# Fused attention and mixture of experts: tables ahead of scatters, maxima transposed in score banks, other places and another engine for weight loads, later last logits

## The chip, the cores and the metric

The kernel runs on one core of a Trainium2 chip, as one program from the attention's inputs to the mixture's output. The metric is the device time of one execution in microseconds (us), taken over several runs of the same kernel. The engines are named as in the profile: PE (TensorE, with PEld for its weight loads), DVE (VectorE), ACT (ScalarE), POOL (GpSimd) and SP (SyncE, which here does little but issue DMAs).

## The reference

```python
scores = (q @ k.T) / sqrt(64)                       # 8 batches, 8 heads, S = 576, D = 64
scores = where(scores >= max(scores) - 0.02, scores, -1e9)
attn = softmax(scores) @ v                          # sum + 1e-9 below
x = attn.transpose(0, 2, 1, 3).reshape(4608, 512)   # tokens x (head, d)
logits = x @ w_gate                                 # 8 experts
e = argmax(logits); gate = softmax(logits)[e]       # one expert per token
for e in range(8):
    h = relu(x[mask_e] @ w1[e])                     # 512 -> 1024
    out[mask_e] = gate * (h @ w2[e])                # 1024 -> 512
```

## The kernel before

**Attention.** The 64 heads are 32 pairs n = 0 to 31, four pairs to a batch b = 0 to 7. Products are exact to about f32 by splitting each f32 operand in two f16 parts (hi, lo) and summing three products. A pair takes NSTEP = 11 steps k. In a step PE makes one score tile `s` (queries on the partitions, for the row maxima, `s_unit`) of a later pair and one transposed score tile `st` (`st_unit`) of the pair at hand, and `av_piece` multiplies masked exponentials with v. `st_unit` makes e = exp on ACT, masks it on DVE, casts it to f16 (`ph`) on ACT and takes the low part (`pl`) on POOL. The maxima of a pair reach the transposed scores through `parts`: DVE reduces them to `r`, PE transposes `r` into a PSUM tile `pst`, ACT and DVE split that in three f16 parts `ptT`, and SP copies them to rows 64 to 66 of the pair's operand tile `CQ`. A pair's operands QK, ck, CQ are in one of four sets, used in turn.

**From attention to experts.** `finish(b)` divides by the sums and writes the tokens of a batch as rows `R`; SP transposes them to `xTg`; `logits(b)` multiplies with the gate's weights (tile `lg`), `route(b)` finds maximum, one-hot expert (`oh`) and the running counts per expert (`run`), all on DVE, and `ranks` places each token by matmuls with `before` and `ones` (`rk`), and POOL scatters the rows by indirect DMA to the table `xs` in DRAM, sorted by expert (`send`). For b = 5, 6, 7 tables follow (`tables0`, `tables1`, `tables2`: counts `cnt`, places `row`, from PE's `pc`), then `fetch(m)` gathers 128 rows of an expert by an indirect DMA on POOL (`Rm`, `spare`, later `R`) and transposes them by a DMA on SP (`xTm`). `lg`, `pst`, `rk`, `pc` all stand in one PSUM bank, tile "m" of the pool `ps_m`; score tiles, and the identity products `hi_v`, `hi_w` that help splitting, use the pool `ps_sc` (tile "sc", six banks).

**Experts.** Weights come in as f32 chunks `wf` (e, w, c) of 512 KB (`load_w`; w = 0 or 1 for w1 or w2, c = 0 to 3), eight for an expert, and `split_w` makes hi and lo parts `wb1`, `wb2` with ACT (hi) and DVE (lo). `gemm1` gives h = relu(x w1) in 96 matmuls of 128 columns for a block of 128 tokens, split in `hl` (ACT, DVE); `gemm2` gives y in 24 matmuls of 512 columns, scaled by the gate (`o`, ACT) and scattered to the output by POOL. Expert 0 (e0) has four early blocks, m = 0 to 3, whose tokens come from batches 0 to 6; m = 3 and 4 sit in the tile `spare`.

**What sets the order.** The Python loop over k writes the instructions; `plan(k, f)` puts an action at a step, `after(k, f)` at so many steps from now, `chain` spreads a list of small operations over steps (or keeps it in one step with `at_once`), `hurry` raises its priority. Pieces of the gemms are mixed into the attention's steps from step KM = KEND - km at the share rate / 100 a step, then one a step from KEND = 352; `moe(c, ready, f)` runs loads, splits and fetches at a chunk number c of that stream. Then a scheduler with a simulated timeline orders each engine's instructions by priority; what is marked `keep_in_program_order` keeps its place. The table TUNE holds the numbers: `lg7` the steps from the last batch's rows to its logits, `w1a`, `w1b` the chunk at which e1's splits begin and their distance, `w1d` the distance of e1's loads, which `close` begins.

Lines: `parts` 370 to 396, `logits` 551, `route` 576, `ranks` 605, `load_w` 789, `split_w` 804, `fetch` 822, `tables0` to `tables2` 1048 to 1063, `close` 1083, the plan of e0's loads and splits 1090 to 1097.

Of the kernel before, what the change touches and what calls it, by code (L numbers as in the profile page):

```python
# [9 lines left out]
F16 = mybir.dt.float16  # L10
# [7 lines left out]
P = 128  # L18
# [26 lines left out]
TUNE = dict(  # L45
    lead=10, cast=2, sl=8, ll=15, sp0=3, sps=0, lv=-16, sv0=-6, sv1=2, av=2, g=4, l=3, d=4, g5=4, l5=3, d5=2, g6=1, l6=2, d6=2, g7=1, l7=1, d7=1, off=2, off5=1, off6=5, lg=4, lg7=14, km=16, rate=15, dh=1, do=3, ws0=6, wsd=2, w1d=5, plv=1, xv=5, so=0, sto=0, ord=0, sc=6, fa=3, fd=4, wa1=-70, wa2=-86, wl1=-28, wl2=-6, avb=1, route=1, ranks=7, pp=8, ew=4, maskat=0, w1a=-42, w1b=5,
)
# [3 lines left out]
def kernel(  # L51
# [55 lines left out]
    NQ = 4  # L107
    cks = [[cpool.tile([P, S], F16, name=f"ck_{i}_{a}") for a in range(2)] for i in range(NQ)]
    cqs = [op.tile([P, 9 * P], F16, tag=f"CQ{i}", name=f"CQ_{i}", bufs=1) for i in range(NQ)]
    none = before[96:96 + NM, 0:64]  # L110
# [80 lines left out]
    def after(k, f, where=END):  # L191
        plan(now[0] + k, f, where)
# [177 lines left out]
    def parts(n):  # L370
# [18 lines left out]

# [186 lines left out]
    def route(b, n, dist, Lj, w, got):  # L576
# [28 lines left out]
        def ranks(dist=dist):  # L605
# [441 lines left out]

    def tables0():
        T[0] = level("0", ((), EARLY[0]), None)
        for m in range(NF):  # L1050
            after(1 + m, lambda m=m: fetch(m))

    def tables1():
        T[1] = level("1", EARLY, T[0])
        for m in range(2):
            after(1 + m, lambda m=m: fetch(NF + m))

    def tables2():
        cnt, s_e = level("2", (EARLY[1], None), T[1])
# [246 lines left out]
```

## Time and profile before

| | us |
|---|---|
| median of 3 runs | 1001.75 (998.88 to 1005.34) |
| the profiled execution | 997.49 |
| its span in the trace | 995.8 |
| PE busy | 941.6 (95% of the span) |
| DVE, ACT, POOL busy | 700.4, 654.1, 563.1 |
| mean granted PE clock | 0.983 of full speed |

Attention runs to about 585 us and the experts to the end; from about 540 to 660 us they overlap, and batches 6 and 7 are routed. Times in the trace are microseconds from the span's start. An idle time in brackets is that of the engine just before the instruction, with what released it. The rows are below.

### The profile page before, as it was taken

The numbers are of one execution on the slowest core, as the hardware profiler recorded it, in microseconds if no ns is written. First come the engines' busy times: TensorE is split into PE (matmuls) and PEld (weight loads), VectorE is DVE, ScalarE is ACT, GpSimd is POOL, SyncE is SP. The second block draws the span as 40 slices with busy tenths as digits, with TensorE's granted clock in tenths as the row PEclk, the third lists the DMA queues.
The fourth block names the chain that finished last, engine by engine and source line by source line (L and its number), as shares of the span: only waits on it lengthen the run. The fifth ranks groups of instructions, "written<-read, shape, count | busy, mean of one in ns | idle before, by whom it ended". The sixth has DMA issues, their size and how long they took to land. (4 is left out here: it accounts for less than half of the span.)

```text
span 995.8 us, 28654 instructions
## 1 busy us (share of the span) xinstructions
PE 941.6 (95%) x11548; PEld 606.9 (61%) x11548; DVE 700.4 (70%) x1413; ACT 654.1 (66%) x1114; POOL 563.1 (57%) x470
## 2 busy tenths in 40 slices
PE   7899999999999999999998998799999999999997
PEld 2355556556566555565664675677666776667684
DVE  7899999989999889999999664816342333423560
ACT  2689897988989888989989853534243332433651
POOL 6366886895986977969969851343122121221121
PEclk8899999999999999999999899999999999999999
DMA  7553454464555646546636569998664756556630
GB/s 199 146 137 75 140 141 134 121 170 113 148 153 137 160 96 175 146 113 161 150 91 193 88 171 276 379 188 247 170 218 116 224 151 180 164 156 214 217 109 27
DMA packets 142750, 159.20 MB, mean 160 GB/s; under 512 B 96403, under 2 KB 112789, under 8 KB 142614
## 3 DMA queue, kind: packets, MB, share of 16 engines
q1 hardware_dynamic: 126598, 100.33, 39.9%
q0 software_dynamic: 9248, 29.45, 9.1%
q10 hardware_dynamic: 6768, 27.55, 8.8%
q8 instruction: 92, 1.51, 0.6%
q14 instruction: 44, 0.36, 0.1%
HBM read 90.24 MB, written 19.44 MB: 110 GB/s over the span
## 5 line engine op out<-in xcount | busy, mean ns | idle before, releaser
L430 POOL TENSOR_TENSOR pl<-e,ph 128x1024 f16<-128x1024 f32 x158 | 335.8, 2133 | 102.3 <-ACT ph L429 64.0
L421 ACT ACTIVATE e<-st,ntau 128x512 f32<-128x512 f32 (+1 forms) x352 | 222.7, 649 | 53.0 <-PE st L405 49.2
L424 DVE SCALAR_TENSOR_TENSOR e<-st,e 128x512 f32<-128x512 f32 (+1 forms) x352 | 220.3, 636 | 11.2 <-ACT e L421 10.5
L947 PE MATMUL y<-wb,hl 128*128 128x512 f16 (+1 forms) x1056 | 202.9, 361 | 0.0
L368 DVE TENSOR_REDUCE nm<-s 128x1 f32<-128x512 f32 x300 | 188.4, 633 | 20.4 <-PE s L358 18.4
L914 PEld LDWEIGHTS <-wb 128*128 128x128 f16 x2304 | 189.4, 98 | 19.8 <-issue 1.5
L914 PE MATMUL h<-xTm,wb 128*128 128x256 f16 (+2 forms) x2112 | 194.7, 253 | 1.0 <-DMA xTm<-Rm 1.0
L474 PE MATMUL av<-vop,ph 128*128 128x65 f16 (+3 forms) x3072 | 187.9, 195 | 2.3 <-ACT x L484 2.0
L474 PEld LDWEIGHTS <-ph 128*128 128x128 f16 (+1 forms) x3072 | 158.8, 100 | 46.4 <-issue 21.7
L474 PE MATMUL av<-vop,pl 128*128 128x65 f16 (+1 forms) x1536 | 167.8, 194 | 5.4 <-POOL pl L430 5.2
L429 ACT CAST ph<-e 128x1024 f16<-128x1024 f32 x160 | 166.3, 1039 | 6.1 <-DVE e L424 5.7
L474 PEld LDWEIGHTS <-pl 128*128 128x128 f16 (+1 forms) x1536 | 137.1, 100 | 37.0 <-issue 11.2
L947 PEld LDWEIGHTS <-hl 128*128 128x128 f16 (+1 forms) x1056 | 94.2, 100 | 98.6 <-issue 3.0
L817 DVE SCALAR_TENSOR_TENSOR wb<-wf,wb 128x1024 f16<-128x1024 f32 x88 | 103.9, 1221 | 56.3 <-ACT wb L809 54.8
L404 PE MATMUL st<-QK 128*128 128x512 f16 (+3 forms) x640 | 139.3, 296 | 1.5 <-DVE lo L255 0.8
L405 PE MATMUL st<-CQ,ck 128*128 128x512 f16 (+3 forms) x640 | 137.8, 290 | 0.5 <-DMA CQ<-ptT 0.5
L356 PE MATMUL s<-QK 128*128 128x512 f16 (+1 forms) x600 | 129.1, 292 | 2.9 <-DMA QK<-hi 2.1
L358 PE MATMUL s<-ck,CQ 128*128 128x512 f16 (+1 forms) x600 | 127.6, 288 | 1.5 <-DMA CQ<-hi 1.5
L961 POOL DMA_INDIRECT out_dram<-o,gt x40 | 47.8, 1194 | 138.6 <-ACT o L958 128.1
L809 ACT ACTIVATE wb<-wf 128x1024 f16<-128x1024 f32 x96 | 98.0, 1050 | 35.5 <-DMA wf<-in_w_dram 18.6
L902 ACT ACTIVATE hl<-h 128x512 f16<-128x512 f32 (+1 forms) x80 | 45.8, 572 | 109.9 <-PE h L914 108.3
L865 DVE COPY gt<-R 128x1 f32<-128x1 f32 x33 | 5.0, 153 | 129.7 <-DMA out_dram<-o,gt 112.5
(195 smaller groups left out, 1018.4 us busy)
## 6 DMA issues: line engine op xcount, KB each, us to landing
wf<-in_w_dram SPq DMA_DIRECT2D x96, 512.0 KB
qkf<-in_qk_dram ACTq DMA_DIRECT2D x30, 576.0 KB
vf<-in_v_dram ACTq DMA_DIRECT2D x15, 640.0 KB
QK<-hi SPq DMA_DIRECT2D x64, 144.0 KB
QK<-lo SPq DMA_DIRECT2D x64, 72.0 KB
QK<-hi SPq DMA_DIRECT2D x64, 72.0 KB
ck<-lo SPq DMA_DIRECT2D x64, 72.0 KB
CQ<-hi SPq DMA_DIRECT2D x64, 64.0 KB
```

The costliest lines, as they stand in the source:

```text
L356: nc.tensor.matmul(sc[rows, oc], d["QA"][a][:, cols], d["KB"][a][:, CH[c]], start=True, stop=False)
L358: nc.tensor.matmul(sc[rows, oc], d["CQ"][:, at:at + cols.stop - cols.start], d["CK"][a][:, CH[c]], start=False, stop=True,)
L368: nc.vector.tensor_reduce(o, sc[:, 0:width(t)], axis=AX.X, op=ALU.max, negate=True)
L404: nc.tensor.matmul(sc[rows, oc], d["KB"][a][:, cols], d["QA"][a][:, CH[c]], start=True, stop=False)
L405: nc.tensor.matmul(sc[rows, oc], d["CK"][a][:, cols], d["CQ"][:, q], start=False, stop=True)
L421: nc.scalar.activation(pf, sc, AF.Exp, bias=ntau, scale=0.125 / SS)
L424: nc.vector.scalar_tensor_tensor(pf, sc, 0.0, pf, ALU.is_ge, ALU.mult)
L429: nc.scalar.copy(h, pd)
L430: (nc.vector if (n, t) in PLV else nc.gpsimd).tensor_tensor(l, pd, h, ALU.subtract)
L474: nc.tensor.matmul(av[:, 0:D] if z == 2 else av, l if z == 1 else h, vop[:, tv, W:W + D] if z == 2 else vop[:, tv, 0:W], start=i in (0, NT ...
L914: nc.tensor.matmul(o, Wt[:, c, wh, f], x, start=c == 0 and z == 0, stop=c == 3 and z == 2,)
L947: nc.tensor.matmul(o, h[:, hh], Wt[:, f, wh, c], start=f == 0 and z == 0, stop=f == 7 and z == 2)
```

## The change

- **TUNE**: `lg7` 14 to 22 (the last batch's logits eight steps later), `km` 16 to 12 and `rate` 15 to 40 (where and how thickly gemm pieces are mixed into attention's last steps), `w1d` 5 to 4, `w1a` -42 to -38, `w1b` 5 to 4.
- **Operand sets**: the four `ck` and four `CQ` tiles become two tiles each of two sets (`ck2`, `cq2`), so that one tile is large enough for a 512 KB chunk.
- **Maxima**: the last two pairs transpose into a score bank (`ps_sc`) and not bank "m"; for the last pair the chain follows in the same step and with priority.
- **Tables**: `ranks` calls `tables0` and `tables1` five steps after it, ahead of part of the scatters, with a lag so that the fetches stay behind; the last batch's `ranks` come 6 steps after `route`, not at once.
- **Loads**: e0's last two chunks of w2 go into the operand sets of pairs 28 and 29 (`ck2[0]`, `cq2[0]`) and are planned at steps 332 and 333; its w2 splits at steps 353, 355, 357, 359 (before 353, 355, 361, 364). ScalarE issues e1's eight loads, SP the others.

```diff
-lg7=14, km=16, rate=15, w1d=5, w1a=-42, w1b=5
+lg7=22, km=12, rate=40, w1d=4, w1a=-38, w1b=4
...
+    ck2 = [cpool.tile([P, 2, 2, S], F16, name=f"ck_{i}") for i in range(NQ // 2)]
+    cq2 = [op.tile([P, 2, 9 * P], F16, tag=f"CQ{i}", name=f"CQ_{i}", bufs=1) for i in range(NQ // 2)]
...
-            ps = ps_m.tile([P, 512], F32, tag="m", name=f"pst_{n}")
+            pool, tag = (ps_sc, "sc") if n >= NPAIR - 2 else (ps_m, "m")
+            ps = pool.tile([P, 512], F32, tag=tag, name=f"pst_{n}")
...
-            chain(1, [
+            chain(int(n < NPAIR - 1), [
...
-            ])
+            ], n == NPAIR - 1)
...
-        (after if n >= 1 else lambda k, f: hurry(f)())(1, turn)
+        if n == 0:
+            hurry(turn)()
+        else:
+            after(1, hurry(turn) if n == NPAIR - 1 else turn)
...
-                after(wait + dist * n, TABLES[b])
+                at = 5 if b < B - 1 else wait
+                after(at, lambda: TABLES[b](wait + dist * n - at))
...
-        after(0 if b == B - 1 else RK[b], ranks)
+        after(6 if b == B - 1 else RK[b], ranks)
...
+        if (e, w) == (0, 1) and c >= 2:
+            wf = (ck2, cq2)[c - 2][0]
...
+            wq[e, w, c] = wf = wf.bitcast(F32)[:, 0:F]
+            nc.sync.dma_start(wf, w12[e, :, c, w])
+            return
...
-            load = nc.sync.dma_start(wf, w12[e, :, c, w])
+            load = (nc.scalar if e == 1 else nc.sync).dma_start(wf, w12[e, :, c, w])
...
-            after(1 + m, lambda m=m: fetch(m))
+            after(lag + 1 + m, lambda m=m: fetch(m))
...
-        t = k + WS0 + WSD * i if i < 4 else KEND + (1, 3, 9, 12)[i - 4]
+        t = k + WS0 + WSD * i if i < 4 else KEND + 1 + 2 * (i - 4)
...
+            plan(NSTEP * (NPAIR - 2) + i - 4, lambda i=i: load_w(*wseq[i]))
-    TABLES = {B - 3: hurry(tables0), B - 2: tables1, B - 1: tables2}
+    TABLES = {B - 3: tables0, B - 2: tables1, B - 1: tables2}
```

**Place 1, PE where the last pair's maxima are transposed.** Before, `pst_31` stands behind 59 matmuls of `av_29_0`, with score tiles 2 and 3 of pair 30 well ahead of it:

```order
L474 LDWEIGHTS pl_29_2_11930
L474 MATMUL av_29_0_12357<-vop_0_127,pl_29_2_11930 128x65
L474 LDWEIGHTS ph_29_2_11929
L474 MATMUL av_29_0_12357<-vop_0_127,ph_29_2_11929 128x64
L379 MATMUL pst_31_12343<-ident_94,r_31_12326 9x128
L474 LDWEIGHTS ph_29_8_12002
L474 MATMUL av_29_1_12553<-vop_0_127,ph_29_8_12002 128x65
```

Now it stands behind 22 matmuls of `av_29_0`, and pair 30's score tiles 2 and 3 come after it:

```order
L480 MATMUL av_29_0_12355<-vop_0_119,ph_29_0_11901 128x65
L480 LDWEIGHTS pl_29_0_11902
L480 MATMUL av_29_0_12355<-vop_0_119,pl_29_0_11902 128x65
L382 MATMUL pst_31_12335<-ident_94,r_31_12318 9x128
L410 LDWEIGHTS QK_30_0_11134
L410 MATMUL st_30_2_12345<-QK_30_0_11134 128x512
L411 LDWEIGHTS ck_1_116
L411 MATMUL st_30_2_12345<-CQ_1_118,ck_1_116 128x512
L410 LDWEIGHTS QK_30_0_11134
L410 MATMUL st_30_3_12371<-QK_30_0_11134 128x512
```

The transpose moved forward by 37 matmuls of `av_29_0` and by score tiles 2 and 3 of pair 30, which now stand behind it. The first half of `lg_6` (24 matmuls), which stood after score tile 9 of pair 30, now stands ahead of it, right behind score tile 1.

**Place 2, SP where e0's last and e1's loads were.** The names are `wf_` expert, chunk, w1 or w2 (0 or 1). Before:

```order
L794 DMA wf_0_2_1_12999<-in_w12_dram 128x1024
L794 DMA wf_0_3_1_13052<-in_w12_dram 128x1024
L794 DMA wf_1_0_0_13373<-in_w12_dram 128x1024
L860 DMA_TRANSPOSE spare_13218<-spare_13218 128x8x128 x2
L860 DMA_TRANSPOSE xTm_5_13555<-Rm_5_13554 128x8x128
L860 DMA_TRANSPOSE xTm_6_13890<-Rm_6_13889 128x8x128
L543 DMA_TRANSPOSE xTg_7_0_13430<-R_129 128x8x128 x2
L794 DMA wf_1_1_0_13469<-in_w12_dram 128x1024
L543 DMA_TRANSPOSE xTg_7_2_13473<-R_129 128x8x128 x2
L543 DMA_TRANSPOSE xTg_7_4_13506<-R_129 128x8x128
L794 DMA wf_1_2_0_13546<-in_w12_dram 128x1024
L794 DMA wf_1_3_0_13572<-in_w12_dram 128x1024
```

Now, from the fetches of blocks 3 and 4 (`spare`) to the first load of e2:

```order
L873 DMA_TRANSPOSE spare_13240<-spare_13240 128x8x128
L549 DMA_TRANSPOSE xTg_7_0_13444<-R_121 128x8x128 x2
L873 DMA_TRANSPOSE spare_13240<-spare_13240 128x8x128
L873 DMA_TRANSPOSE xTm_5_13543<-Rm_5_13542 128x8x128
L549 DMA_TRANSPOSE xTg_7_2_13491<-R_121 128x8x128 x2
L549 DMA_TRANSPOSE xTg_7_4_13520<-R_121 128x8x128
L873 DMA_TRANSPOSE xTm_6_13774<-Rm_6_13773 128x8x128
L807 DMA wf_2_0_0_13674<-in_w12_dram 128x1024
```

No load stands between the transposes any more; e0's last two chunks stand further ahead in SP's row, right behind `xTg_6_0`, and e1's are with ACT, between the operations of batch 7's rows:

```order
L807 DMA wf_1_1_0_13463<-in_w12_dram 128x1024
L822 ACTIVATE wb1_1_13390<-wf_1_0_0_13393 128x1024
L915 ACTIVATE hl_2_0_13468<-h_2_0_13397 128x512
L541 CAST R_121<-xn_7_2_13440 128x4x128
L541 CAST R_121<-xn_7_3_13461 128x4x128
L915 ACTIVATE hl_2_0_13468<-h_2_1_13471 128x512
L822 ACTIVATE wb1_1_13390<-wf_1_1_0_13463 128x1024
L541 CAST R_121<-xn_7_4_13487 128x4x128
L807 DMA wf_1_2_0_13534<-in_w12_dram 128x1024
L807 DMA wf_1_3_0_13557<-in_w12_dram 128x1024
L807 DMA wf_1_0_1_13573<-in_w12_dram 128x1024
L971 ACTIVATE o_0_0_13575<-y_0_0_13538,gt_0_0_12521 128x512
```

Each load of e1 now stands behind ACT's own work ahead of it, no more behind SP's transposes.

**Place 3, DVE where the last batch is routed.** `lg_7` to `run` is the route of batch 7, `wb2_1` the splits of e1's w2, `wb1_0` those of e2's w1. Before:

```order
L593 TENSOR_TENSOR ex_7_13746<-lg_7_13599,mx_7_13743 128x40
L903 SCALAR_TENSOR_TENSOR hl_3_0_13784<-h_3_0_13663,hl_3_0_13784 128x512
L817 SCALAR_TENSOR_TENSOR wb2_1_13371<-wf_1_2_1_13741,wb2_1_13371 128x2x512
L594 TENSOR_TENSOR lg_7_13599<-lg_7_13599,rank8_108 128x40
L817 SCALAR_TENSOR_TENSOR wb1_0_11668<-wf_2_0_0_13782,wb1_0_11668 128x1024
L595 TENSOR_REDUCE mw_7_13744<-lg_7_13599 128x5
L903 SCALAR_TENSOR_TENSOR hl_3_0_13784<-h_3_1_13787,hl_3_0_13784 128x512
L817 SCALAR_TENSOR_TENSOR wb2_1_13371<-wf_1_3_1_13887,wb2_1_13371 128x2x512
L596 TENSOR_TENSOR oh_7_13745<-lg_7_13599,mw_7_13744 128x40
L817 SCALAR_TENSOR_TENSOR wb1_0_11668<-wf_2_1_0_13899,wb1_0_11668 128x1024
L598 TENSOR_REDUCE lg_7_13599<-oh_7_13745 128x8
L602 TENSOR_TENSOR run_114<-run_114,lg_7_13599 128x8
```

Now:

```order
L830 SCALAR_TENSOR_TENSOR wb2_1_13391<-wf_1_2_1_13614,wb2_1_13391 128x2x512
L830 SCALAR_TENSOR_TENSOR wb1_0_11660<-wf_2_0_0_13674,wb1_0_11660 128x1024
L830 SCALAR_TENSOR_TENSOR wb2_1_13391<-wf_1_3_1_13672,wb2_1_13391 128x2x512
L597 TENSOR_REDUCE mx_7_13820<-lg_7_13692 128x5
L598 TENSOR_TENSOR lg_7_13692<-lg_7_13692,mx_7_13820 128x40
L599 TENSOR_TENSOR ex_7_13823<-lg_7_13692,mx_7_13820 128x40
L600 TENSOR_TENSOR lg_7_13692<-lg_7_13692,rank8_108 128x40
L830 SCALAR_TENSOR_TENSOR wb1_0_11660<-wf_2_1_0_13797,wb1_0_11660 128x1024
L601 TENSOR_REDUCE mw_7_13821<-lg_7_13692 128x5
L602 TENSOR_TENSOR oh_7_13822<-lg_7_13692,mw_7_13821 128x40
L604 TENSOR_REDUCE lg_7_13692<-oh_7_13822 128x8
L608 TENSOR_TENSOR run_114<-run_114,lg_7_13692 128x8
```

The route's operations now stand nearly together, with one split between them instead of five and two `hl`; but all of them stand behind the last split of e1's w2 (`wf_1_3_1`).

On PE the 60 matmuls of `lg_7` stand 15 matmuls of y (512 columns) and 60 of h (128 columns) later among the gemms. On POOL, fetches 0 and 1 stand ahead of two `pl` operations instead of behind them, and the first fetches into `R` stand behind the outputs of blocks 3 and 4, before only behind that of block 3. All engines keep their order in the attention's steady state and after the eighth block's h.

## Rows read from the trace of the kernel before

**Rows 1.** The profile's page, part 1: busy time, share of the span, instructions.

```profile
PE 941.6 (95%) x11548; PEld 606.9 (61%) x11548; DVE 700.4 (70%) x1413; ACT 654.1 (66%) x1114; POOL 563.1 (57%) x470
```

**Rows 2.** Windows: stretch, us, busy (x) of PE, PEld, DVE, ACT, POOL, PEclk, DMA, GB/s.

```profile
530.00:549.00 19.00, 14.70 (x226) 9.03 (x227) 17.16 (x42) 18.20 (x35) 18.54 (x15) 1.00 0.65 177
549.00:556.00 7.00, 6.63 (x99) 4.47 (x99) 4.50 (x15) 4.03 (x10) 6.52 (x5) 0.51 0.68 110
...
577.00:601.00 24.00, 22.21 (x342) 17.71 (x341) 17.74 (x42) 11.40 (x24) 9.88 (x10) 1.00 0.73 169
601.00:628.00 27.00, 19.32 (x238) 12.92 (x237) 12.94 (x20) 12.79 (x16) 3.99 (x4) 0.93 1.03 329
628.00:660.00 32.00, 32.00 (x350) 23.27 (x347) 21.09 (x75) 11.27 (x20) 13.54 (x17) 0.95 0.98 301
660.00:996.00 336.00, 329.14 (x2543) 229.74 (x2541) 127.41 (x167) 131.03 (x173) 77.50 (x96) 1.00 0.57 169
```

**Rows 3.** Timeline of PE: start, us, engine, line, work, [idle before <-releaser].

```profile
539.39 0.38 PE L405 MATMUL st<-CQ,ck 128*128 128x512 f16 x1
...
544.40 0.20 PE L474 MATMUL av<-vop,pl 128*128 128x65 f16 x1 [0.94 <-POOL pl L430]
...
547.36 0.28 PE L379 MATMUL pst<-ident,r 128*9 128x128 f32 x1 [0.94 <-DVE row L658]
...
549.37 0.69 PE L254 MATMUL hi_v<-vop,ident_h 128*128 128x320 f16 x2 [1.34 <-ACT vop L286]
...
560.75 0.83 PE L914 MATMUL h<-xTm,wb 128*128 128x128 f16 x12 [1.03 <-DMA xTm<-Rm]
...
588.35 0.59 PE L254 MATMUL hi_w<-wb,ident_h 128*128 128x512 f16 x2 [1.79 <-ACT wb L809]
...
604.09 0.48 PE L561 MATMUL lg<-wg,xTg 128*128 128x8 f16 x12 [2.66 <-DMA xTg<-R]
...
620.85 1.84 PE L914 MATMUL h<-spare,wb 128*128 128x128 f16 x30
627.71 0.19 PE L610 MATMUL rk<-oh,before 128*128 128x8 f16 x1 [5.02 <-DVE run L602]
...
633.43 0.17 PE L663 MATMUL pc<-run,ones 128*128 128x8 f16 x1
...
660.15 2.06 PE L914 MATMUL h<-xTm,wb 128*128 128x128 f16 x34
```

**Rows 4.** Timeline of DVE at the last pair's maxima and ahead of block 4.

```profile
544.25 0.17 DVE L375 TENSOR_REDUCE r<-nm 128x9 f32<-128x18 f32 x1
...
547.12 0.18 DVE L658 CAST row<-pc 128x32 int32<-128x32 f32 x1
...
617.97 1.23 DVE L817 SCALAR_TENSOR_TENSOR wb<-wf,wb 128x1024 f16<-128x1024 f32 x1 [0.68 <-ACT wb L809]
```

**Rows 5.** Timeline of POOL: two `pl`, a fetch behind them, first fetch to `R`.

```profile
548.63 4.20 POOL L430 TENSOR_TENSOR pl<-e,ph 128x1024 f16<-128x1024 f32 x2
553.00 1.01 POOL L850 DMA_INDIRECT Rm<-xs,row  x1 [0.16 <-issue]
...
646.14 0.99 POOL L850 DMA_INDIRECT R<-xs,row  x1 [4.97 <-DVE at_e L745]
```

**Rows 6.** Timeline of SP's DMA queue: weight loads from 577 us on.

```profile
577.60 5.34 SPq L794 DMA_DIRECT2D wf<-in_w_dram  x3
...
603.54 0.54 SPq L794 DMA_DIRECT2D wf<-in_w_dram  x1
...
608.99 3.47 SPq L794 DMA_DIRECT2D wf<-in_w_dram  x4
```

**Rows 7.** Windows of PE for line 947 (y), then for line 914 (h).

```profile
615.60:620.90 5.30, 5.23 (x24) 2.31 (x24) 1.00 1.02 394
...
588.70:594.10 5.40, 5.32 (x96) 5.32 (x95) 1.00 0.58 146
```

More of the change, by code (lines that the diff above doesn't have):

```diff
@@ L45 @@
 TUNE = dict(
-    lead=10, cast=2, sl=8, ll=15, sp0=3, sps=0, lv=-16, sv0=-6, sv1=2, av=2, g=4, l=3, d=4, g5=4, l5=3, d5=2, g6=1, l6=2, d6=2, g7=1, l7=1, d7=1, off=2, off5=1, off6=5, lg=4, lg7=14, km=16, rate=15, dh=1, do=3, ws0=6, wsd=2, w1d=5, plv=1, xv=5, so=0, sto=0, ord=0, sc=6, fa=3, fd=4, wa1=-70, wa2=-86, wl1=-28, wl2=-6, avb=1, route=1, ranks=7, pp=8, ew=4, maskat=0, w1a=-42, w1b=5,
+    lead=10, cast=2, sl=8, ll=15, sp0=3, sps=0, lv=-16, sv0=-6, sv1=2, av=2, g=4, l=3, d=4, g5=4, l5=3, d5=2, g6=1, l6=2, d6=2, g7=1, l7=1, d7=1, off=2, off5=1, off6=5, lg=4, lg7=22, km=12, rate=40, dh=1, do=3, ws0=6, wsd=2, w1d=4, plv=1, xv=5, so=0, sto=0, ord=0, sc=6, fa=3, fd=4, wa1=-70, wa2=-86, wl1=-28, wl2=-6, avb=1, route=1, ranks=7, pp=8, ew=4, maskat=0, w1a=-38, w1b=4,
 )
@@ L107 @@
     NQ = 4
-    cks = [[cpool.tile([P, S], F16, name=f"ck_{i}_{a}") for a in range(2)] for i in range(NQ)]
-    cqs = [op.tile([P, 9 * P], F16, tag=f"CQ{i}", name=f"CQ_{i}", bufs=1) for i in range(NQ)]
+    ck2 = [cpool.tile([P, 2, 2, S], F16, name=f"ck_{i}") for i in range(NQ // 2)]
+    cq2 = [op.tile([P, 2, 9 * P], F16, tag=f"CQ{i}", name=f"CQ_{i}", bufs=1) for i in range(NQ // 2)]
+    cks = [[ck2[i // 2][:, i % 2, a] for a in range(2)] for i in range(NQ)]
+    cqs = [cq2[i // 2][:, i % 2] for i in range(NQ)]
     none = before[96:96 + NM, 0:64]
@@ L791, in load_w @@
         i = int(e != 0)
+        if (e, w) == (0, 1) and c >= 2:
+            wf = (ck2, cq2)[c - 2][0]
+            wf = wf.rearrange("p a b s -> p (a b s)") if c == 2 else wf.rearrange("p a s -> p (a s)")
+            wq[e, w, c] = wf = wf.bitcast(F32)[:, 0:F]
+            nc.sync.dma_start(wf, w12[e, :, c, w])
+            return
         wq[e, w, c] = wf = pools[i].tile([P, F], F32, tag="wf", name=f"wf_{e}_{c}_{w}", bufs=2 + 6 * i)
         if e in range(E):
-            load = nc.sync.dma_start(wf, w12[e, :, c, w])
+            load = (nc.scalar if e == 1 else nc.sync).dma_start(wf, w12[e, :, c, w])
             if e == 1:
@@ L1046, in level, with tables0, tables1, tables2 @@
         return cnt, s_e
-    def tables0():
+    def tables0(lag):
         T[0] = level("0", ((), EARLY[0]), None)
         for m in range(NF):
-            after(1 + m, lambda m=m: fetch(m))
-    def tables1():
+            after(lag + 1 + m, lambda m=m: fetch(m))
+    def tables1(lag):
         T[1] = level("1", EARLY, T[0])
         for m in range(2):
-            after(1 + m, lambda m=m: fetch(NF + m))
-    def tables2():
+            after(lag + 1 + m, lambda m=m: fetch(NF + m))
+    def tables2(lag):
         cnt, s_e = level("2", (EARLY[1], None), T[1])
@@ L1092 @@
     for i in range(8):
-        t = k + WS0 + WSD * i if i < 4 else KEND + (1, 3, 9, 12)[i - 4]
+        t = k + WS0 + WSD * i if i < 4 else KEND + 1 + 2 * (i - 4)
         plan(t, lambda i=i: split_w(*wseq[i]))
-        if i + 2 < 8:
+        if i < 4:
             plan(t, lambda i=i: load_w(*wseq[i + 2]))
-    TABLES = {B - 3: hurry(tables0), B - 2: tables1, B - 1: tables2}
+        elif i >= 6:
+            plan(NSTEP * (NPAIR - 2) + i - 4, lambda i=i: load_w(*wseq[i]))
+    TABLES = {B - 3: tables0, B - 2: tables1, B - 1: tables2}
     plan(KEND + 12, close)
```

## The prediction

> **What bounds the kernel now.** I read the page's busy times first: TensorE is busy 941.6 of the span's 995.8 us, and no other engine comes near [rows 1]. So a change pays only where TensorE stands still or runs at a lower clock. The windows say where that is. From 660 us on TensorE is busy 329.14 of 336 us at full clock, and the change moves nothing there. From 530 to 660 us, where attention ends, the experts begin and the last batches are routed, it is busy 14.70 of 19 us, 6.63 of 7 at a granted clock of 0.51, 22.21 of 24, and 19.32 of 27 at 0.93 [rows 2]. The change touches this stretch alone. In TensorE's timeline I then read what released each long wait there: 0.94 us for `pl`, 0.94 for the table's `row`, 1.34 for `vop`, 1.03 for `xTm`, 1.79 for `wb`, 2.66 for `xTg` and 5.02 for `run` [rows 3]. That is 13.7 us. The clock adds, by (1 - clock) times length, 0.49 x 7 = 3.4 us at 549 to 556, 0.07 x 27 = 1.9 at 601 to 628 and 0.05 x 32 = 1.6 at 628 to 660 [rows 2]: 6.9 us. The ceiling of what can be gained is 20.6 us.
>
> **Maxima in a score bank, tables ahead.** `pst_31` waits 0.94 us for `row`, not for its input: `r` is reduced at 544.25 us and `row`, which ends the use of bank "m" by the table, at 547.12 [rows 3, 4]. In a score bank this wait goes. What is late next is `r` itself: the new order puts the transpose behind 22 rather than 59 matmuls of `av_29_0`, and the DVE operations of the table ahead of `r` are 11 instead of 5, about 0.2 us each, so `r` comes about a microsecond later in its row. Also `lg_6` now uses bank "m" earlier, and may wait for `row`. And the `pl` behind the first wait is POOL's pace: POOL is busy 18.54 of 19 us [rows 2], and two fetches of about 1 us now stand ahead of 4.20 us of `pl`, not behind them [rows 5]. So of the 3.2 us of waits here (0.94 + 0.94 + 1.34) I can bound the gain only by 0 and 3.2 and take the middle, **1.6 us**. The half clock at 549 to 556 follows these waits; if they shrink it may not fall. It is worth 0 to 3.4; I take the middle, **1.7**.
>
> **Fetches earlier.** The first fetches stand 4.20 us of `pl` earlier [rows 5], more than the 1.03 us that h then waits for `xTm` [rows 3]. I take **1.0 us** (0 to 1.03); the 4.20 us is what hides it.
>
> **e0's last weights in operand sets.** Before, these chunks have to wait for one of two `wf` buffers, and SP issues them at 577.60 us [rows 6]; the split of the last one comes just before the 1.79 us wait for `wb` at 588.35 [rows 3]. The sets of pairs 28 and 29 come free when pair 29's last scores are done, at 539.39 + 0.38 us [rows 3], some 38 us earlier, so the data is there before ScalarE can split it. I take **1.8 us** (0 to 1.8); it would be nothing if ScalarE's own queue, not the data, held the split, which its 11.40 busy us of 24 make unlikely [rows 2].
>
> **Last logits later.** `lg_7` stands 15 matmuls of y and 60 of h later. A y takes 5.23 / 24 = 0.218 us and an h 5.32 / 96 = 0.055 us [rows 7], so 3.3 + 3.3 = 6.6 us of work now run ahead of the logits, against a wait of 2.66 us for `xTg` [rows 3]. The wait goes, and with it probably the lower clock of this stretch: **2.66 + 1.9 = 4.6 us** (0 to 4.6).
>
> **The loads of e1 and the last route.** The long wait is that of `rk` for `run`, 5.02 us [rows 3]. Two things make `run` late, just ahead of 627.71 us [rows 3]: the route's ten small operations stand between five splits of 1.2 us, and these splits are late because the weights are. SP issued e1's first chunk in the row of three at 577.60 to 582.9, the second at 603.54 and four more at 608.99, since they stood behind transposes that wait for rows [rows 6]. Now ScalarE issues them, the second behind a `hl` and the casts of batch 7's first rows, some 5 to 8 us earlier, and the route stands together, but behind the last split of e1's w2. Logits 6.6 us later push `run` back, splits 5 to 8 us earlier pull it forward, and what stands between is 1.2 us instead of about 7.5. Meanwhile TensorE loses less ahead of it and so comes to `rk` earlier. Bounds: 0 if `run` moves with TensorE, 5.02 + 1.6 = 6.6 if it is early. I take half, **3.3 us**. ScalarE's eight issues, at about the 0.54 us of the single one in SP's row [rows 6], are up to 4.3 us of its time, hidden as long as it is busy 11.40 of 24 and 12.79 of 27 us [rows 2]; without that cover they would be on the path of `hl`.
>
> A rule of the Trainium skill speaks against this part: its page "DMA: Bandwidth & Descriptors", section "Issuing engines are not separate DMA queues", says that DMAs started by different engines run on the same 16 DMA engines and interleave, so that issuing from several saves only the sequencer's time to start them. By it alone this term would be near nothing and the sum 9.7. The trace agrees that the engines are full (a share of 1.03 at 601 to 628 [rows 2]), but the loads before were late in a queue in order, which the rule does not speak of.
>
> **New waits.** In the new order 21.4 us of TensorE's work lie between the last `pc` and the first h on blocks fetched into `R` (before: 633.43 to 660.15 us, 26.7 [rows 3]). The fetch began 12.7 us after that `pc`, at 646.14 [rows 5], and the data is in place some 8 us later (5 blocks' fetches and two transposes): 20.7 us. Slack is 0.7 us, and the fetch now stands behind one more output, which waits for a y that ends 10.4 us after `pc`. I take **-1.0 us** (0 to -3.5), with the waits of `lg_6` for its transposes in it.
>
> **Sum.** 1.6 + 1.7 + 1.0 + 1.8 + 4.6 + 3.3 - 1.0 = 13.0 us. The profiled execution took 997.49 us with its span of 995.8, so 984.5. The median of the runs shown, 1001.75, is 4.3 us above it; so I predict **989 us** as a median.
>
> **Rivals.** (A) The sum as above. (B) The wait only moves. h of block 4 starts at 620.85 without a wait, and the split ahead of it ends at 619.2 [rows 3, 4]: 1.65 us of slack. If TensorE gains 8 us ahead of it and e1's loads come no earlier, since DMA is full at 1.03 [rows 2], h waits there for `wb` and `rk` behind it: the terms 4.6 and 3.3 shrink to about 1, the gain is 3 to 9, and the time about 996. For it: the share of 1.03. Against: the loads are spread over a longer stretch, 0.73 at 577 to 601. (C) No change: POOL, at 18.54 of 19, and ScalarE, at 18.20 of 19 [rows 2], set the pace up to 549 us, and later waits come back as others; 1002, within 3. (D) Slower: the gap before the h on `R`. It decides where the chain `rk`, scatter, table, fetch, which lasts 646.14 - 627.71 = 18.4 us [rows 3, 5], starts late: with logits 6.6 us later and the route behind e1's last split, itself up to 6 us late when DMA is full, less the 0.7 us of slack, TensorE stands 12 us and the clock falls for about the 7 us at 0.51 seen once (3.4 us). If the other terms give 3, the time is 1001.75 + 12 + 3.4 - 3 = 1014. With all terms of A in place it decides only from 13 us of standing on. Against: TensorE has 21.4 us of work there.
>
> By the rule of the page named above, B would be the outcome: e1's data lands no earlier.
>
> **Chances and range.** A 0.60, B 0.20, C 0.13, D 0.05, and 0.02 for more than the ceiling. Two runs of this kernel lie up to 0.6% apart, so 1% (991.7 and 1011.8) is about what a measurement can tell from no change. All but a little of A lies below 991.7: faster 0.60, with some of B's best edge in place of A's worst; B, C and the better side of D within 1%: 0.34; slower 0.06. The lower end is the ceiling, 1001.75 - 20.6 = 981, and 980 with the spread; the upper end takes in B and half of C: 1000.
>
> **What would show it.** In the changed kernel's trace: `pst` no longer released by `row`; `xTm`, `hi_w` and `lg_7` without waits over 0.5 us; e1's loads in ScalarE's queue, the second before 600 us; `rk` waiting less than 3 us, with a clock near 1.00 in the stretch; the first h on `R` waiting under 2 us; the time from that h to the end unchanged, 996 - 660 = 336 us. I am wrong if `rk` still waits 5 us (B), if the waits at 540 to 556 keep their sum (C), or if the h on `R` waits over 5 us (D).

## The result, and the profile after

The changed kernel is slower: a median of 1016.1 us (1012.64 to 1020.0, 6 runs) against 1002.43 (998.88 to 1007.37, 6 runs) of the kernel before, a ratio of 1.0134 with a 95% interval of 1.0097 to 1.0172. Two later comparisons of the same two kernels gave 1.0117 (1.0064 to 1.0169) and 1.0102 (1.0040 to 1.0164). The forecast was 989 us, faster, in a range of 980 to 1000.

The profiled execution took 1016.57 us with a span of 1014.8, 19.0 more than the span of before. All of it arises between 600 and 700 us. The windows of the changed kernel, with the columns of [rows 2]:

```profile
601.00:628.00 27.00, 21.32 (x263) 14.71 (x261) 7.30 (x8) 6.72 (x8) 2.98 (x3) 0.94 1.13 216
628.00:660.00 32.00, 23.70 (x241) 16.64 (x242) 22.99 (x74) 14.20 (x22) 9.15 (x8) 0.84 0.76 287
660.00:700.00 40.00, 34.32 (x299) 24.53 (x297) 11.15 (x24) 9.62 (x14) 14.01 (x20) 0.91 0.84 188
700.00:1014.00 314.00, 308.14 (x2327) 212.68 (x2325) 119.81 (x156) 122.90 (x162) 65.08 (x86) 1.00 0.55 165
```

PE, which was busy 32.00 of 32 us at 628 to 660 [rows 2], is now busy 23.70 of 32 and 34.32 of 40. At 601 to 628 the DMA engines are busier than before (a share of 1.13, before 1.03) and move less: 216 GB/s, before 329. PE's timeline shows the waits that answer to [rows 3], and the blocks of h and y behind them:

```profile
545.59 0.24 PE L480 MATMUL av<-vop,pl 128*128 128x65 f16 x1 [1.85 <-POOL pl L436]
546.78 0.40 PE L382 MATMUL pst<-ident,r 128*9 128x128 f32 x1
...
616.27 0.48 PE L567 MATMUL lg<-wg,xTg 128*128 128x8 f16 x12 [2.92 <-DMA xTg<-R]
...
634.95 0.19 PE L616 MATMUL rk<-oh,before 128*128 128x8 f16 x1 [9.72 <-DVE lg L604]
...
657.58 4.95 PE L927 MATMUL h<-xTm,wb 128*128 128x128 f16 x83
662.84 0.44 PE L927 MATMUL h<-xTm,wb 128*128 128x128 f16 x5 [0.31 <-issue]
...
665.06 0.27 PE L927 MATMUL h<-xTm,wb 128*128 128x128 f16 x2 [1.09 <-issue]
...
666.57 0.59 PE L960 MATMUL y<-wb,hl 128*128 128x512 f16 x2
...
674.96 3.12 PE L927 MATMUL h<-xTm,wb 128*128 128x128 f16 x53
```

`rk` starts 7.2 us later than in [rows 3] (634.95 for 627.71), having waited 9.72 us for DVE instead of 5.02. The first h on `R` starts 14.8 us later (674.96 for 660.15), so another 7.6 us are lost between the two, and 4.2 us behind it. About 7.0 of these 11.8 us are no wait that the profile can name: in h of blocks 5, 6 and 7, and once in y, PE pauses ("issue"). Block 6 takes 666.57 - 657.58 = 8.99 us for its 96 matmuls, which [rows 7] do in 5.32. Most of the rest goes with the granted clock, 0.84 at 628 to 660 us and 0.91 at 660 to 700 (before 0.95 and 1.00): it fell to its half level (1.2 of 2.4 GHz) during the wait for `rk` and after the pauses of blocks 6 and 7. By (1 - clock) times length that is 5.1 + 3.6 = 8.7 us, before 1.6, though a part of it falls on PE's own waiting.

Why DVE was late is read backwards. The route's first operation (`mx`) follows two splits that DVE could begin only at 629.77, when ScalarE had its halves, and ScalarE had waited 6.72 us for a chunk (ACTq are the loads that ScalarE issues):

```profile
629.77 2.36 DVE L830 SCALAR_TENSOR_TENSOR wb<-wf,wb 128x1024 f16<-128x1024 f32 x2 [6.55 <-ACT wb L822]
632.05 0.19 DVE L597 TENSOR_REDUCE mx<-lg 128x5 f32<-128x40 f32 x1
...
634.73 0.16 DVE L608 TENSOR_TENSOR run<-run,lg 128x8 f16<-128x8 f16 x1
```

```profile
596.93 1.06 ACT L822 ACTIVATE wb<-wf 128x1024 f16<-128x1024 f32 x1 [1.50 <-DMA wf<-in_w_dram]
...
598.51 1.67 ACTq L807 DMA_DIRECT2D wf<-in_w_dram  x3
...
602.59 1.06 ACT L822 ACTIVATE wb<-wf 128x1024 f16<-128x1024 f32 x1 [1.61 <-DMA wf<-in_w_dram]
603.29 0.33 ACTq L807 DMA_DIRECT2D wf<-in_w_dram  x1
606.25 1.06 ACT L822 ACTIVATE wb<-wf 128x1024 f16<-128x1024 f32 x1 [2.61 <-DMA wf<-in_w_dram]
...
628.68 2.95 ACT L822 ACTIVATE wb<-wf 128x1024 f16<-128x1024 f32 x3 [6.72 <-DMA wf<-in_w_dram]
```

By the order of the program those two splits on DVE are `wb1_0<-wf_2_0_0`, of e2's first chunk, and `wb2_1<-wf_1_3_1`, of e1's last, both ahead of `mx_7` (place 3 above). The chunk that was late is e2's: the last packet of ScalarE's loads ended at 624.8 us, about 4 us before ScalarE went on. e2's chunk is loaded by SP. Here is SP's queue of the changed kernel (the time is from the first issue of a row to the end of its last, so it is how long SP is held, not how long the data travels):

```profile
592.43 4.26 SPq L549 DMA_TRANSPOSE xTg<-R  x2
...
599.49 12.06 SPq L549 DMA_TRANSPOSE xTg<-R  x3
611.65 4.11 SPq L873 DMA_TRANSPOSE xTm<-Rm  x1
616.30 18.14 SPq L807 DMA_DIRECT2D wf<-in_w_dram  x10
```

and of the kernel before, at the same work:

```profile
600.79 2.66 SPq L543 DMA_TRANSPOSE xTg<-R  x2
...
604.17 4.77 SPq L543 DMA_TRANSPOSE xTg<-R  x3
```

The last three transposes of batch 7's rows hold SP for 12.06 us instead of 4.77, and one of block 6 for 4.11, while loads of ScalarE are in flight. These are at most three chunks at once: the first two had been split by 596.93, three were issued at 598.51, and the next at 603.29, when the third had been split. So the rows come late to the logits, and e2's first load is not issued before 616.30.

### The profile page after: what moved, and what is told of

It reads as the page before. It is cut to its first block, busy times and chain, and to the rows that moved or that the text cites. A ratio compares the mean times of both kernels' runs of the same rounds, so it can differ in the third digit from the quotient of the medians.

```text
span 1014.8 us, 28646 instructions
## 1 busy us (share of the span) xinstructions
PE 949.3 (94%) x11548; PEld 610.5 (60%) x11548; DVE 699.2 (69%) x1413; ACT 653.9 (64%) x1114; POOL 558.2 (55%) x470
## 5 line engine op out<-in xcount | busy, mean ns | idle before, releaser
L927 PEld LDWEIGHTS <-wb 128*128 128x128 f16 x2304 | 191.5, 99 | 31.5 <-issue 13.0
L927 PE MATMUL h<-xTm,wb 128*128 128x256 f16 (+2 forms) x2112 | 200.3, 254 | 8.7 <-issue 8.6
L960 PE MATMUL y<-wb,hl 128*128 128x512 f16 (+1 forms) x1056 | 205.2, 364 | 0.8 <-issue 0.8
L974 POOL DMA_INDIRECT out_dram<-o,gt x40 | 43.4, 1085 | 167.5 <-ACT o L971 149.3
L822 ACT ACTIVATE wb<-wf 128x1024 f16<-128x1024 f32 x94 | 95.9, 1051 | 37.1 <-DMA wf<-in_w_dram 19.3
L971 ACT ACTIVATE o<-y,gt 128x512 f32<-128x512 f32 (+1 forms) x40 | 26.6, 664 | 101.0 <-PE y L960 80.0
```

Source lines behind the costliest of these rows:

```text
L927: nc.tensor.matmul(o, Wt[:, c, wh, f], x, start=c == 0 and z == 0, stop=c == 3 and z == 2,)
L960: nc.tensor.matmul(o, h[:, hh], Wt[:, f, wh, c], start=f == 0 and z == 0, stop=f == 7 and z == 2)
```

## The experiments

Each kernel is compared with the kernel before on the same chip, side by side; "the full change" is the changed kernel. Five groups of runs were made, each on a chip of its own.

### First group: which part does it

**u_sp**, the full change with e1's loads on SP again:

```diff
-            load = (nc.scalar if e == 1 else nc.sync).dma_start(wf, w12[e, :, c, w])
+            load = nc.sync.dma_start(wf, w12[e, :, c, w])
```

> The changed kernel with e1's loads issued by SP again. Theory 1 (the route waits for the split of e2's first chunk, whose load comes late): the row of DVE still has that split ahead of the route, so rk still waits 7 us or more, and the time stays within 4 us of 1016. Rival 1 (ScalarE's issuing is what makes the weights late): the wait of rk falls to 5 us or less and the time to about 1010 or below.

Measured: 1002.71 us against 1001.04, a ratio of 1.0011 (0.9993 to 1.0030). The loss is gone with this one line, so the rival that blames ScalarE's issuing holds for the time. Theory 1 holds for the place of the wait: it is still 7.19 us, as the route still stands behind the splits.

```profile
629.73 0.19 PE L616 MATMUL rk<-oh,before 128*128 128x8 f16 x1 [7.19 <-DVE run L608]
```

```profile
603.66 5.06 SPq L549 DMA_TRANSPOSE xTg<-R  x3
608.82 4.59 SPq L807 DMA_DIRECT2D wf<-in_w_dram  x7
613.52 6.25 SPq L873 DMA_TRANSPOSE xTm<-Rm  x1
```

The transposes take 5.06 us again, and the loads start behind them. The transpose of block 6, which now stands behind seven loads of SP's own queue, holds SP 6.25 us: loads delay a transpose from this queue too, and what the order saves are the rows of batch 7.

**u_lg14**, the full change with `lg7=14`.

> The changed kernel with the last logits at the old place (lg7 back to 14), all else as changed. Theory 1: in the changed kernel rk waits 9.72 us because the last route stands on DVE behind the splits of e1's last chunk and of e2's first, whose load SP issues only at 616.3 us, behind transposes. Here the route begins ahead of the last two e1 splits in DVE's row, but its last operations still stand behind the split of e2's first chunk: the wait falls to about 6 us and the time by 3 to 5 us, to about 1012. Rival 1: what is late is e1's weights themselves, since ScalarE's loads and SP's share the same DMA engines: then the wait moves to the h of block 4 or stays near 10 us, and the time stays at 1016 within 3.

Measured: 1006.74 us, 1.0067 (1.0045 to 1.0090). This is a smaller loss than the full change has, and below what either theory gave. In its trace the logits wait 8.13 us for `xTg`, which neither theory had said, and `rk` 5.45; but that trace is of the longest of the five runs, 1015.32 us where the other four took 1005.71 to 1007.91.

**u_tune**, the full change with the old table of numbers:

```diff
-lg7=22, km=12, rate=40, w1d=4, w1a=-38, w1b=4
+lg7=14, km=16, rate=15, w1d=5, w1a=-42, w1b=5
```

> The changed kernel with the table of numbers of the kernel before; the maxima in score banks, the early tables, the chunks in operand sets and ScalarE's loads stay. Here the route stands in DVE's row ahead of all splits of e2 and of three of e1. Theory 1: rk waits 4 us or less, and the time is 1000 or below, since the earlier parts of the change gained 2.7 us by the second block's h. Rival 1 (ScalarE's loads are late whatever the order): rk waits 5 us or more and the time is 1005 to 1015. The short pauses of PE in h without a releaser (13 us in the changed kernel): if they belong to the changed order of the splits and loads they are gone here, and if they belong to ScalarE's queue they stay.

Measured: 1013.88 us, 1.0151 (1.0115 to 1.0188). Theory 1 fell as the cause of the loss: here `rk` waits for nothing over 0.6 us, and the logits wait 4.25, 4.89 and 3.68 us for `xTg` instead. The time is the one that rival 1 gave, though not with its wait at `rk`. What is common is that transposes are late.

**b_again**, the kernel before, for a second trace.

> The kernel before once more, for its trace. Theory 2: the pauses of PE of 0.3 to 1.1 us in h without a releaser (13 us in the changed kernel, none in the first trace of before) belong to the changed kernel: none here, span within 3 us of 996. Rival 2: they come and go from execution to execution: some of them here too, and a span several us longer.

Measured: span 1002.4. It has pauses in block 6: rival 2, so the first trace of before was one without them (more below).

### Second group: single parts on the kernel before

**b_act**, the kernel before with ScalarE issuing e1's loads, and nothing else.

> The kernel before with one edit: ScalarE issues e1's eight loads. Theory 3 (formed from the runs with and without this edit on the changed kernel, 1016 and 1003): loads in a second queue run beside the transposes of batch 7's rows, which stand in SP's row, and delay them; SP's single queue had kept the loads behind them. Then the logits of batch 7 wait for xTg by 8 us or more in all, the second transpose to the last takes over 4 us to land where it took 2 to 3, and the time is 1008 to 1016. Rival 3 (the edit hurts only with the changed places of the last logits and of the splits): time within 4 us of 1001.

Measured: 1007.04 us against 1000.27, 1.0047 (1.0016 to 1.0079), between the two ranges. The edit alone costs, less than within the full change. PE's, SP's and ACT's rows show where:

```profile
607.23 0.48 PE L561 MATMUL lg<-wg,xTg 128*128 128x8 f16 x12 [5.66 <-DMA xTg<-R]
...
621.09 0.48 PE L561 MATMUL lg<-wg,xTg 128*128 128x8 f16 x12 [6.91 <-DMA xTg<-R]
```

```profile
597.97 9.04 SPq L860 DMA_TRANSPOSE xTm<-Rm  x1
607.10 1.26 SPq L543 DMA_TRANSPOSE xTg<-R  x1
```

```profile
595.37 0.82 ACTq L794 DMA_DIRECT2D wf<-in_w_dram  x2
...
605.93 1.06 ACT L809 ACTIVATE wb<-wf 128x1024 f16<-128x1024 f32 x1 [8.58 <-DMA wf<-in_w_dram]
...
606.89 0.60 ACT L535 CAST R<-xn 128x512 f16<-128x512 f32 x1
```

One transpose of a block holds SP 9.04 us, where its neighbour takes 1.26, with two chunks of ScalarE in flight; the rows of batch 7 stand behind it. The next of them has a second reason to be late: the cast that makes it, at 606.89, stands in ACT's row behind a split that waited 8.58 us for its load. `rk` then waits for nothing, where it waited 5.02 us before, so not all of the delay adds to the time.

**u_sp_tune**, the full change with the loads on SP and the old numbers.

> The changed kernel with e1's loads on SP and the old table of numbers: what is left are the maxima in score banks, the early tables, the chunks in operand sets and the later ranks of batch 7. Theory: these parts gain what the milestones show up to the first h of the experts (2.7 us), and rk waits about 4 us, as before: 996 to 999. Rival: the gain is given back at 563 to 570 us, where VectorE's pl of 1.2 us lasts 5.2 to 5.6 us beside two pl of GpSimd back to back, and in pauses of PE: 1000 to 1003.

Measured: 1001.76 us, 1.0009 (0.9980 to 1.0039): the rival. The other parts of the change together neither gain nor lose what can be measured.

**b_lg22**, the kernel before with `lg7=22`.

> The kernel before with the last batch's logits eight steps later (lg7=22) alone. The prediction's term: the wait of 2.66 us for xTg goes and the time falls by 2.7 to 4.6 us, to about 997. Theory 1: the wait only moves to rk, as the route now stands behind the splits of e1's last chunk and e2's first: rk waits 7 us or more, and the time is 1000 to 1004.

Measured: 1003.2 us, 1.0017 (0.9982 to 1.0051). Theory 1 holds here: the logits wait less, and `rk` takes it over.

```profile
608.17 0.46 PE L561 MATMUL lg<-wg,xTg 128*128 128x8 f16 x12 [1.15 <-DMA xTg<-R]
...
627.74 0.19 PE L610 MATMUL rk<-oh,before 128*128 128x8 f16 x1 [9.02 <-DVE run L602]
```

**b_pst**, the kernel before with the last maxima in score banks.

> The kernel before with the last two pairs' maxima transposed in score banks, and the last pair's chain hurried, alone. The prediction's term: the wait of 0.94 us of pst for row goes, and 1 to 2 us with it: 999 to 1000. Rival: the next wait, that of av for pl, takes it up, and the time is 1001 within 1; the order of DVE's route and splits also differs a little from the kernel before, so rk's wait may move by 1 us either way.

Measured: 998.18 us, 0.9980 (0.9953 to 1.0007). The direction and size of the prediction's term, but the interval holds 1. No kernel of this study beat the kernel before by more than its interval; this one came nearest.

### Third group: how many loads, and the order of the splits

**a_act_w1** and **a_act_w2**, the full change with only half of e1's loads on ScalarE:

```diff
-(nc.scalar if e == 1 else nc.sync)
+(nc.scalar if (e, w) == (1, 0) else nc.sync)     # a_act_w1; (1, 1) for a_act_w2
```

> The changed kernel, where ScalarE issues only the four loads of e1's w1 and SP the four of w2. Theory 3 (loads in a second queue run beside the transposes of batch 7's rows and delay them): these four are the ones that run beside the transposes, so most of the harm stays: logits wait for xTg by 4 us or more, SP issues the next load late (after 612 us), and the time is 1008 to 1014. Rival 4 (harm comes from the loads of w2, which stand late in ScalarE's row, between splits): 1003 within 3.

> The changed kernel, where ScalarE issues only the four loads of e1's w2 and SP the four of w1. Theory 3: these come behind or at the end of the transposes, so the harm is small: 1002 to 1006, rk waits about 7 us as with all loads on SP. Rival 4: 1010 or more, with w2's last load landing after 620 us.

Measured: 997.04 us, 1.0025 (0.9999 to 1.0052), and 998.35 us, 1.0037 (1.0008 to 1.0065), against 994.85. Theory 3 fell in this form for w1: those loads do run beside the transposes, two chunks at a time, and the last three transposes take

```profile
602.84 6.64 SPq L549 DMA_TRANSPOSE xTg<-R  x3
```

6.64 us, more than 4.77, but not 12.06. The number of chunks at once does not explain it alone: two are in flight here as in b_act, where one transpose took 9.04 us, and three at most in the full change. In a_act_w2, whose loads are issued from 600.33 us on and so mostly behind the transposes, theory 3 gave the size; there `rk` waits 10.25 us, longer than in the full change, at about a fourth of its loss. The wait at `rk` by itself is therefore no measure of the loss.

**c1**, out of the change only the maxima in score banks, the chunks in operand sets and the later ranks, and **c1_w30_6**, the same with `w1a=-30, w1b=6`.

> Out of the changed kernel: maxima in score banks and e0's last chunks in operand sets, with the old table of numbers, the old place of the tables (behind the scatters) and e1's loads on SP. Theory: VectorE's long pl at 563 to 570 us (5.2 to 5.6 us) comes from the early tables, which put GpSimd's two pl back to back against it; without them it lasts 2.5 us or less, and the time is 996 to 999. Rival: it stays, and the time is 1000 to 1002.

> As c1, but e1's splits planned later (w1a -30, w1b 6), so that in DVE's row only one split of e1's w1 and w2 stands between the operations of the last route, before five. Theory 1 (what makes rk wait is the number of splits ahead of and between the route's operations): rk waits 3 us or less, where the kernel before has 5, and the time is 2 to 3 us below c1, about 994 to 996. Rival: the splits that were moved back are now waited for by y of block 4 or h of block 4, and the time is that of c1 within 1 us.

Measured: 995.37 us, 1.0007 (0.9982 to 1.0032), and 996.61, 1.0018 (0.9996 to 1.0039). The kernel before takes 994.85 us on this chip, so the forecasts are read as differences to it: c1 gains nothing, as its rival said, and c1_w30_6 gains nothing over c1, as its rival said for the time but not for the place. In c1 VectorE's `pl` still takes 4.80 us, so it is not the early tables alone that bring it. In c1_w30_6 the order does what it should for `rk`, and the next step of the same chain takes the wait over:

```profile
620.82 0.18 PE L616 MATMUL rk<-oh,before 128*128 128x8 f16 x1 [0.95 <-DVE run L608]
...
629.68 0.17 PE L669 MATMUL pc<-run,ones 128*128 128x8 f16 x1 [4.44 <-DVE posi L625]
```

### Fourth and fifth group: bytes in flight

**a_again**, the full change; **u_sp2**, as u_sp; **a_act_half**, the full change with chunks of half the size on ScalarE:

```diff
+            if e == 1:
+                load = nc.scalar.dma_start(wf[:, 0:512], w12[e, :, c, w, 0:512])
...
+        if e == 1:
+            x = wf[:, 0:512].unsqueeze(1).to_broadcast([P, 2, 512])
```

> The changed kernel once more, beside the others of this call on one chip. Theory 3b (ScalarE's loads in flight beside SP's transposes delay both): 10 to 14 us above u_sp2 of this call, xTg_7 and xTm transposes of 4 to 9 us in SP's queue, rk waiting 9 us. Rival 5 (the harm belongs to the chip of the first call): within 4 us of u_sp2. Pauses of PE in h without a releaser: if they belong to the chip, then all kernels of this call have them (5 to 9 us) or none has.

> The changed kernel with e1's loads on SP once more: within 3 us of the kernel before, whatever the chip; rk waits 5 to 8 us.

> The changed kernel, where ScalarE's eight loads of e1 bring only the first half of each chunk (256 KB for 512; the splits use that half twice, so expert 1 computes with other weights; all else is as changed, but DVE's row puts one more split of e2 ahead of the last route). Theory 3b (bytes in flight beside the transposes): the transposes of xTg and xTm take 1.2 to 3 us in SP's queue again, SP issues e2's first load before 612 us, rk waits 7 us or less, and most of the 13 us goes: 1 to 5 us above u_sp2. Rival 6 (a second ring beside SP's is what costs, whatever the bytes, or the route's place behind the splits of e2): within 4 us of a_again.

Measured on one chip, against 1002.15: 1016.26 us, 1.0117 (1.0064 to 1.0169); 1004.11, 1.0013 (0.9983 to 1.0042); 1003.92, 1.0015 (0.9984 to 1.0046). With half the bytes the loss is gone, though ScalarE issues as many loads in the same queue, and though DVE's row now has three splits of e2 ahead of the route. Rival 6 fell. The last three transposes of batch 7 are quick again and e2's first load goes out at 609.30; the first two take 7.24 us, where the full change has 4.26:

```profile
592.73 7.24 SPq L549 DMA_TRANSPOSE xTg<-R  x2
...
601.41 1.29 SPq L549 DMA_TRANSPOSE xTg<-R  x1
...
604.20 3.27 SPq L549 DMA_TRANSPOSE xTg<-R  x2
609.30 19.87 SPq L810 DMA_DIRECT2D wf<-in_w_dram  x12
```

```profile
627.58 0.19 PE L616 MATMUL rk<-oh,before 128*128 128x8 f16 x1 [6.72 <-DVE run L608]
```

The run changes more than the bytes, though. ScalarE's row of three loads goes out at 604.68 us and not at 598.51, when the first of the last three transposes is through and the second is being issued, and in SP's row block 6's transpose stands ahead of the last two of batch 7 and not behind them. So it shows that a second queue with eight loads does not cost by itself, not that the bytes alone do. `u_sp2` came out as expected, with 5.42 us of waiting at `rk`; in the trace of `a_again`, an execution of 1027.62 us, `rk` waits 2.90 us and not the 9 expected, and the logits wait 10.07 and 4.74 us.

**b_again2**, the kernel before on that chip.

> The kernel before on this chip, for its trace: if the pauses in h belong to the chip, it has them exactly if the other kernels of this call have them.

Measured: span 1000.2, with the pauses, as the other kernels on that chip have them.

**a_third**, the full change, and **a_act_w1b**, as a_act_w1, on one more chip.

> The changed kernel a third time: 10 to 16 us above the kernel before of this call, with transposes of batch 7's rows and of block 6 that take 4 us or more each in SP's queue.

> The changed kernel with only e1's w1 loads on ScalarE, beside the full change on one chip. Theory 3b (bytes in flight beside the transposes: here at most two chunks at once, in the full change four and more): 1 to 4 us above the kernel before, as on the other chip. Rival 5 (the other chip hid it): 8 us or more above the kernel before.

Measured, against 999.99: 1012.74 us, 1.0102 (1.0040 to 1.0164), and 1003.68, 1.0022 (0.9996 to 1.0048). Eight loads cost, and four cost nothing that can be measured, on one chip; rival 5 fell. In the profiled execution of the full change, the longest of its four (1022.13 us), the last three transposes hold SP 16.72 us and the loss stands at the logits as well as at `rk`, which waits 8.09 us:

```profile
605.41 16.72 SPq L549 DMA_TRANSPOSE xTg<-R  x3
```

```profile
622.53 0.48 PE L567 MATMUL lg<-wg,xTg 128*128 128x8 f16 x12 [7.91 <-DMA xTg<-R]
```

So this much is shown: e1's eight loads on ScalarE and not on SP cost 12 us on one chip (1016.26 against 1004.11), and 9 us more than four of them do on another (1012.74 against 1003.68). The traces show the path: transposes that hold SP longer, later logits, a later first load of e2, a later route, and pauses and a lower clock behind it. That it is the bytes in flight is likely, not shown: the run with half the bytes also issues its loads later. A run that holds ScalarE's full loads back until the last transpose is issued would part the two; it was not made. Nor was it tried what in the DMA engines makes a transpose up to seven times longer beside plain loads (9.04 us for 1.26).

## Why the prediction was wrong, point by point

**Maxima and tables (1.6 + 1.7).** `pst` lost its wait for `row`, as said. Its neighbour took it up, as the text had named but not priced: `av` waits 1.85 us for `pl`, before 0.94. The clock's half level did not go: it lies at 544.6 to 551.4 us by the granted clock, before at 549.0 to 555.9. The term of the clock was nothing in this execution; in that of a_third the half level lasts 3.4 us there (544.1 to 547.6), which gives the forecast 1.7.

**A cost not seen.** With the loads on SP, PE stands 3.38 us at 569.69, since VectorE's own `pl`, which takes 1.22 us alone (at 573.25), lasts 5.60. In the trace of u_sp, VectorE, GpSimd and PE:

```profile
563.84 5.60 DVE L436 TENSOR_TENSOR pl<-e,ph 128x1024 f16<-128x1024 f32 x1
```

```profile
561.92 4.22 POOL L436 TENSOR_TENSOR pl<-e,ph 128x1024 f16<-128x1024 f32 x2
...
566.24 2.11 POOL L436 TENSOR_TENSOR pl<-e,ph 128x1024 f16<-128x1024 f32 x1
```

```profile
569.69 0.58 PE L410 MATMUL st<-QK 128*128 128x512 f16 x1 [3.38 <-DVE e L430]
```

It ends 1.1 us after the last of GpSimd's, so it had stood until then. In the trace of before the same operation takes 2.50 us, in the three of the changed kernel 2.39, 5.62 and 5.52. The Trainium skill has the rule, in "SBUF — State Buffer", section "SBUF: two separate sides": VectorE, in an operation with two SBUF inputs, and a GpSimd operation that reads SBUF hold a shared pair of ports exclusively, and the loser stands for the whole instruction. The trace agrees (4.5 us of standing, behind two of GpSimd's operations). It probably eats the gain of the maxima, of `xTm` and of part of `hi_w`: u_sp_tune, where it lasts 5.59 us, gains nothing, but no run takes it away alone.

**Fetches and e0's last weights (1.0 + 1.8).** Right in themselves: neither `xTm` nor `hi_w` is waited for in the changed kernel.

**Last logits (4.6).** This step failed. It took the wait at the logits for the price, but the route behind them runs on DVE, in order, and moving the logits put it behind more splits: alone, the edit takes the wait from 2.66 to 1.15 and moves `rk` from 5.02 to 9.02 (b_lg22), and the time goes from 1000.27 to 1003.2 us, no gain. With it the terms without e1's loads, 9.7 us of gain in the sum, came to nothing: 1.7 and 2.0 us above the kernel before in u_sp and u_sp2, within their intervals.

**Loads of e1 (3.3).** This step failed too, and it turned the sign. I counted how early ScalarE issues the loads and took the earlier landing for a gain on the path. From the second chunk to the sixth they did land earlier (the second is split at 596.93, before at 607.71; the third at 602.59, before at 613.73); but SP's one queue had also kept the loads behind the transposes, and this order was worth more than the waiting it made. Measured on one chip, the term is minus 12 us (1016.26 against 1004.11). The page of the Trainium skill that I weighed, "DMA: Bandwidth & Descriptors", section "Issuing engines are not separate DMA queues", says that DMAs of different engines run on the same 16 DMA engines and interleave, and that issuing from several saves only the sequencer's time. The traces agree with the first: ScalarE's loads and SP's transposes move in the same stretch, at 216 GB/s for 329. By the second the term would have been nothing; the measurement is a loss. I also had "behind the last split of e1's w2" for what the route waits for, when the row printed above it in place 3, a split of e2's first chunk, is loaded by SP behind the very transposes that the change slows.

**New waits (-1.0).** The h on `R`, where rival D lay, does not wait (674.96 has no bracket). D's time, 1014 us, came near the measured one by luck: what it rests on, PE standing ahead of that h, did not happen. Rival B named the right resource, the DMA share over 1, but bounded its price by loads that land no earlier, not by transposes that land later. A rival "transposes slowed by the loads" was missing, although the lg wait of 2.66 us for `xTg` showed that they were on the path.

**From the profile to the median (+4.3).** This gap has a likely cause in the traces: block 6 of before takes 4.7 us longer in its third trace, with pauses of PE and the half clock behind them, and the first trace of before did not have them. The size was right for the kernel before, and 19.0 us of difference between the two profiled spans is 13.7 between medians for this reason; the changed kernel's profiled execution, 1016.57 us, lay at its median.

## What to carry to other kernels

A queue that issues in order is also a priority: before moving loads off it, look at what stands in it behind which, and ask how long the urgent transfers take when the loads run beside them. A wait removed from PE returns at the next instruction that hangs on the same in-order engine; price the whole chain to the last consumer, here logits, route, `rk`, `pc`. And where a profile and the median differ by several us, find the difference in a second trace before using either as a base.

## What the runs showed of the hardware

**Transposes beside loads.** A DMA transpose of 128 rows holds SP 1.25 us when little else is in flight, 9.04 us with two 512 KB loads of ScalarE's queue in flight (b_act), and 6.25 us behind seven loads of its own queue (u_sp). In the changed kernel, at 601 to 628 us, the DMA share is higher than before (1.13 for 1.03) and fewer bytes move (216 GB/s for 329).

**Pauses in h.** PE stops for 0.3 to 1.3 us at steps of about 0.75 us, with no releaser, nearly always in h of 128 columns. In the third trace of before, on the fourth group's chip (b_again2; PE, block 6):

```profile
648.58 2.40 PE L914 MATMUL h<-xTm,wb 128*128 128x128 f16 x40
651.43 0.27 PE L914 MATMUL h<-xTm,wb 128*128 128x128 f16 x2 [0.46 <-issue]
652.93 0.33 PE L914 MATMUL h<-xTm,wb 128*128 128x128 f16 x3 [1.23 <-issue]
...
654.37 4.47 PE L914 MATMUL h<-xTm,wb 128*128 128x128 f16 x50 [0.50 <-issue]
658.63 5.72 PE L947 MATMUL y<-wb,hl 128*128 128x512 f16 x25
```

Block 6 takes 658.63 - 648.58 = 10.05 us, 4.7 more than 5.32. All four kernels of the third group have none, and on that chip the kernel before takes 994.85 us, 5 to 7 less than on the others (999.99 to 1002.15). The first trace of before has none either. Every trace of the other groups has them in block 6, and the changed kernel's three also in block 5. So they seem to go with the chip, which one chip without them does not prove. How full the DMA engines are does not decide it: in the changed kernel PE pauses at 662 to 668 us with a DMA share of 0.85, and at 675.0 to 678.1 it runs 53 matmuls of h without a pause, with a share of 1.09 (674.9 to 678.5). What PE lacks in the pauses the traces don't show, and it stays open.
